# Attention with two gated layers: one line for all transfers in the planner, a later projection of head 1, and 1/z of seven head pairs spread by DMA

## The chip, the core and the metric

The kernel runs on one core of a Trainium2 chip. A core has TensorE (PE in the views; its weight loads are PEld), VectorE (DVE), ScalarE (ACT), GpSimd (POOL) and SyncE (SP), which issues transfers; ScalarE issues transfers as well. The metric is the device time of one execution in microseconds, taken as the median of repeated runs.

## The reference

Two batches of eight attention heads, 768 positions, head dimension 64, all in float32. A query sees a key only where six sign bits of a projection agree. The heads' outputs, side by side, go through two gated feed-forward layers.

```python
q_bits = (np.einsum('bhsd,dk->bhsk', q, proj) > 0)        # six bits
mask = q_bucket[:, :, :, None] == k_bucket[:, :, None, :]
scores = np.where(mask, scale * q @ k.T, -1e9)
attn = np.exp(scores - scores.max(-1, keepdims=True))
attn = attn / (attn.sum(-1, keepdims=True) + 1e-09)        # 1/z of each query
x = (attn @ v) laid out as [batch, seq, 512]
x = spatial_gating(x, w_in, w_spatial, b_spatial, w_out)   # first layer
out = x + relu(layernorm(x) @ w_ch1) @ w_ch2               # second layer
```

## The kernel before

**How work is put in order.** The kernel's code does not issue instructions. Each call (`nc.vector...`, `nc.sync.dma_start`) is recorded as a job in `Plan`, with its engine and what it must come behind. `Plan.run` then gives every job a modelled start, and `Plan.issue` writes the instructions of each engine in the order of these starts. The modelled numbers only set the order: on the chip each engine goes through its own list in order and waits on semaphores for what an instruction really needs. `plan.behind` adds an artificial "not ahead of this job". For transfers the model uses two tables, `LAND` (a fixed time by kind) and `RATE` (bytes per microsecond), and one queue for each of the two issuing engines.

**Stages.** The attention part goes over 96 tiles, each of 128 queries of one head (six tiles a head, two heads a pair, four pairs a batch). `attn_step` writes, for step i: the transposes of tile i (`pt`, six on PE), the scores of tile i+2 (`sc`, eight matmuls on PE: four chunks of two passes), the masked maximum of tile i+1 (`x`, on DVE), its exponent with the row sum z (ACT). A head's six tiles are closed by `po` (PE, weighted values), whose result goes to `xT`, one slice of 128 rows (two heads) by 768 queries for each pair. There are two score buffers in PSUM (`ps_s`) and four buffers for everything else (`ps_b`). `pair_load`, `mismatch` (PE products `pm` with `sides`, then the bits `m` on DVE), `pair_split` and `passes_of` prepare the operands `ks` and `qs` of the next head; `passes_of` puts them together by transfers on SP, partly from `m`. The layers' work is mixed into the last third of the attention part and follows it.

**Normalization.** `summed` takes 1/(z + 1e-9) of a pair in one tile `zr` (128 queries x 12: six query blocks by two heads). `normalized`, three tiles behind the last `po` of the pair, widens `zr` to 128x384 on POOL twice (`zw`), transposes it by six 128x128 matmuls into PSUM (`pz`), and multiplies `xT` by it on DVE, twice 128x384.

**Start.** `sides` holds the signed projection for head 0 in partitions 0 to 63 and for head 1 in 64 to 127, each made by three small DVE instructions from `pj`, loaded on ACT's queue. `mismatch(0, 0, slice(0, D))` projects head 0 alone, `first_parts` builds the operands of the first two query groups, and a second `mismatch(0, 0)` projects the whole pair for head 1. The first is `pm_0_151` and the second `pm_0_179` in the order below (`pm_0_203` after the change).

Of the kernel before, what the change touches and what calls it, by code (L numbers as in the profile page):

```python
# [169 lines left out]
class Plan:  # L170
# [15 lines left out]
    LAND = {"load": 2.0, "move": 1.5, "store": 1.5}  # L186
    RATE = {"load": 300e3, "move": 195e3, "store": 200e3}
# [111 lines left out]
    def run(self, late=None):  # L299
# [10 lines left out]
        queue = {e: 0.0 for e in engines}  # L310
# [42 lines left out]
        while todo:  # L353
# [38 lines left out]
            if j.bytes:  # L392
                other = "ACT" if e == "SP" else "SP"
                begin, span = max(queue[e], free[e] + self.LAND[j.way]), j.bytes / self.RATE[j.way]
                both = max(0.0, min(queue[other] - begin, 2 * span)) / 2
                if both:
                    queue[other] += both
                j.end = queue[e] = begin + span + both
# [113 lines left out]
def attn_moe_kernel(ctx: ExitStack, tc: tile.TileContext, qT, kT, v, proj, w_in, w_spT, b_sp, w_out, g_ln, w1, w2, out):  # L512
# [103 lines left out]
    nc.scalar.dma_start(out=pj[0:D], in_=proj)  # L616
    nc.scalar.dma_start(out=pj[D:P], in_=proj)
# [6 lines left out]
    for a, own in enumerate((slice(0, D), slice(D, P))):  # L624
        for i, sign in enumerate((1.0, -1.0, 1.0)):
            at = a * HROW + i * NB
            nc.vector.tensor_scalar(sides[own, at : at + NB], pj[own], sign, None, op0=ALU.mult)
    side = {"k": sides[:, NB : NB + QUAD], "q": sides[:, 0:QUAD]}
# [202 lines left out]
    def scores(b, h, g, j):  # L831
        jm = f"{b}_{h}_{g}_{j}"
        ks, qs = heads[b, h]["ks"], groups[b, h, g]["qs"]
        qsl = slice(j * P, (j + 1) * P)
        sc = ps_s.tile([P, 1024], F32, tag="sc", name=f"sc_{jm}")[:, :S]
        for csl in (slice(0, 512), slice(512, S)):
            for i, rows in enumerate((P, MR)):
                nc.tensor.matmul(
                    sc[:, csl], qs[:rows, i, qsl], ks[:rows, i, csl], start=(i == 0), stop=(i == 1)
                )  # L840
        tiles[b, h, g, j] = {"sc": sc}

    def masked_max(b, h, g, j):
# [15 lines left out]
        if (b, h, g, j) == (0, 0, 0, 0):  # L859
            pair_split(0, 0, first=True)  # L860
# [41 lines left out]
    def summed(b, r):  # L902

        zr = ap.tile([P, NQT, 2], F32, tag="zr", name=f"zr_{b}_{r}")
        nc.vector.tensor_scalar(zr, z_sum[b][:, :, 2 * r : 2 * r + 2], 1e-9, None, op0=ALU.add)
        nc.vector.reciprocal(zr, zr)
        pairs[b, r]["zr"] = zr

    def normalized(b, r):

        zr = pairs[b, r]["zr"]
        for c in range(2):
            zw = ap.tile([P, 6, D], F32, tag="zw", name=f"zw_{b}_{r}_{c}", bufs=2)
            zc = zr[:, c * 3 : c * 3 + 3, :].rearrange("p a (h o) -> p (a h) o", o=1)
            nc.gpsimd.tensor_scalar(zw, zc.to_broadcast([P, 6, D]), 1.0, 0.0, op0=ALU.mult, op1=ALU.add)
            pz = ps_b.tile([P, 3, P], F32, tag="b", name=f"pz_{b}_{r}_{c}")
            for i in range(3):
                nc.tensor.transpose(pz[:, i, :], zw[:, 2 * i : 2 * i + 2].rearrange("p h d -> p (h d)"), ident)
            xs = xT[b][:, r, c * KC : (c + 1) * KC]
            nc.vector.tensor_tensor(xs, pz.rearrange("p a n -> p (a n)"), xs, op=ALU.mult)  # L920

    def attn_step(i):
# [758 lines left out]
```

## Time and profile before

| | |
|---|---|
| median of 3 runs | 646.48 us (645.09 to 646.70) |
| time of the profiled execution | 645.79 us |
| its span, first to last instruction | 643.6 us |
| PE busy | 634.8 us (99%) |
| DVE busy | 500.4 us (78%) |
| ACT busy | 327.7 us (51%) |
| POOL busy | 189.6 us (29%) |

The profile is of one execution. The 2.2 us between its span and its time lie before the first and behind the last instruction. Nearly all instructions are recorded through one helper, so they carry one source line (L502) and are told apart by the names of their tiles, written out<-in.

### The profile page before, as it was taken

How to read it: one execution, taken by the hardware profiler on the slowest of the kernel's cores; microseconds unless marked ns; L12 is line 12 of the kernel's file. 1: busy time of each engine (PE TensorE's matmuls, PEld its weight loads, DVE VectorE, ACT ScalarE, POOL GpSimd, SP SyncE). 2: the span in 40 equal slices, each digit the busy share in tenths (PEclk: the TensorE clock that was granted, in tenths of full speed). 3: DMA queues.
4: the chain of work that ended last, by engine and by line, in shares of the span. 5: the costliest groups of instructions: out<-in, count | busy, mean ns of one | idle time of the engine just before them, and what ended most of it. 6: DMA issues, size and time to landing. Idle time of an engine off the chain costs nothing.

```text
span 643.6 us, 10095 instructions
## 1 busy us (share of the span) xinstructions
PE 634.8 (99%) x3506; PEld 520.3 (81%) x3506; DVE 500.4 (78%) x998; ACT 327.7 (51%) x650; POOL 189.6 (29%) x186
## 2 busy tenths in 40 slices
PE   7999999999999999999999999999999999999997
PEld 5777767777787777877888888899999899898896
DVE  6789878797888686886799544699998887969555
ACT  7888877885565655643555323554323333333110
POOL 2142433244554633131343200122122324142200
PEclk9999999999999999999999999999999999999999
DMA  6776676667767877774653240421262626382623
GB/s 153 195 206 155 181 181 154 183 145 240 204 181 243 235 195 212 228 264 176 231 167 145 73 148 17 147 86 46 99 231 114 234 92 223 105 279 74 218 88 143
DMA packets 64738, 107.68 MB, mean 167 GB/s; under 512 B 7008, under 2 KB 33328, under 8 KB 64432
## 3 DMA queue, kind: packets, MB, share of 16 engines
q1 hardware_dynamic: 43232, 67.58, 36.0%
q10 hardware_dynamic: 21456, 39.46, 18.5%
q8 instruction: 28, 0.46, 0.3%
q14 instruction: 22, 0.18, 0.1%
HBM read 63.31 MB, written 24.90 MB: 137 GB/s over the span
## 4 chain that ended last, share of the span: by engine, by line
PE 94%; DMA 2%; DVE 2%; issue 1%; SPq 0%; POOL 0%; ACTq 0%; DVEq 0%; POOLq 0%
PE acc L502 20%; PE p L502 14%; PE pv L502 10%; PE sc L502 10%; PE pt L502 10%; PE po L502 9%; PE pg L502 7%; PE pc L502 5%; PE py L502 5%; DMA qs<-q 2%; PE pm L502 1%; PE pz L502 1%; PE ptr_g L502 1%; PE px_c L502 1%; DMA pj<-in_proj 1%
## 5 line engine op out<-in xcount | busy, mean ns | idle before, releaser
L502 PE MATMUL acc<-w,ch 128*128 128x512 f32 x576 | 142.9, 393 | 0.0
L502 PEld LDWEIGHTS acc<-w,ch 128*128 128x128 f32 x576 | 107.3, 188 | 18.9
L502 ACT ACTIVATE x<-x,nb 128x768 f32<-128x768 f32 x96 | 89.7, 936 | 31.3 <-DVE x L502 26.4
L502 DVE TENSOR_SCALAR_CACHE_REDUCE x<-sc 128x768 f32<-128x768 f32 x96 | 90.9, 951 | 6.8 <-PE sc L502 3.7
L502 PE MATMUL sc<-ks,qs 128*128 128x512 f32 (+3 forms) x384 | 93.8, 363 | 1.9 <-DVE x L502 1.2
L502 POOL TENSOR_TENSOR f64c_w<-f_w,f64c_w 128x512 f32<-128x512 f32 x32 | 44.1, 1380 | 152.9 <-issue 81.8
L502 PE MATMUL pt<-ident,x 128*128 128x128 f32 x576 | 81.3, 274 | 0.3 <-DVE xT L502 0.3
L502 PEld LDWEIGHTS pt<-ident,x 128*128 128x128 f32 x576 | 66.5, 140 | 14.9 <-issue 2.4
L502 PEld LDWEIGHTS sc<-ks,qs 128*128 128x128 f32 (+1 forms) x384 | 62.9, 190 | 13.9 <-issue 2.2
L502 PE MATMUL po<-e,vv 128*64 128x384 f32 x384 | 65.5, 490 | 0.0
L502 ACT ACTIVATE ch<-u 128x384 fp32r<-128x384 f32 x48 | 25.2, 525 | 79.1 <-DVE u L502 67.0
L502 ACT ACTIVATE e<-pt 128x384 f32<-128x384 f32 x120 | 55.0, 485 | 18.6 <-PE pt L502 18.1
L502 DVE TENSOR_TENSOR u<-p,u 128x384 f32<-128x384 f32 x84 | 45.4, 552 | 20.5 <-PE p L502 20.0
L502 PEld LDWEIGHTS po<-e,vv 128*64 128x64 f32 x384 | 26.1, 137 | 31.2 <-issue 29.8
L502 PE MATMUL p<-t,w 128*128 128x384 f32 x252 | 50.0, 337 | 0.0
L502 PE MATMUL p<-xh,w 128*128 128x384 f32 x252 | 48.8, 338 | 0.0
L502 DVE COPY e<-pt 128x384 f32<-128x384 f32 x72 | 39.7, 553 | 9.6 <-PE pt L502 9.0
L502 PEld LDWEIGHTS p<-t,w 128*128 128x128 f32 x252 | 44.9, 188 | 2.3
L502 PEld LDWEIGHTS p<-xh,w 128*128 128x128 f32 x252 | 44.6, 188 | 2.2 <-DVE u L502 0.3
L502 POOL TENSOR_TENSOR w<-f64c_w,w 128x512 fp32r<-128x512 f32 (+1 forms) x28 | 35.2, 1259 | 37.8 <-ACT w L502 15.0
L502 DVE TENSOR_SCALAR f64c_w<-f64c_w 128x512 f32<-128x512 f32 x64 | 30.8, 480 | 18.5 <-ACT f64c_w L502 15.8
L502 PE MATMUL pg<-vn,w_sp 128*128 128x512 f32 x180 | 43.6, 396 | 0.0
(155 smaller groups left out, 1018.5 us busy)
## 6 DMA issues: line engine op xcount, KB each, us to landing
f_w<-in_w ACTq DMA_DIRECT2D x32, 512.0 KB
ots<-y_dram SPq DMA_DIRECT2D x12, 768.0 KB
ks<-k SPq DMA_DIRECT2D x45, 192.0 KB
y_dram<-ots SPq DMA_DIRECT2D x30, 256.0 KB
qs<-q SPq DMA_DIRECT2D x30, 192.0 KB
wst_sp<-in_w_spT SPq DMA_DIRECT2D x12, 384.0 KB
vv<-in_v SPq DMA_DIRECT2D x16, 192.0 KB
qs<-q SPq DMA_DIRECT2D x30, 96.0 KB
```

The costliest lines, as they stand in the source:

```text
L502: res = getattr(getattr(nc, engine[j.engine]), op)(*map(live, args), **{k: live(x) for k, x in kw.items()})
```

## The change

It has three parts.

1. In the planner, the two queues of transfers become one line that all transfers go through, with new fixed times and rates and a minimum of 0.1 us each. No instruction comes or goes by this; the order changes on every engine.
2. At the start, `sides` of head 1 is made behind the bits of head 0, and the second `mismatch(0, 0)` is recorded behind the scores of tile 1.
3. For seven of the eight pairs, `zr` is transposed as it is (one matmul, 12 rows by 128), copied to SBUF on DVE (`zt`), stored to DRAM (`zd`, 6 KB) and loaded again twice, each time one row of 768 spread over 64 partitions (`zb`, 192 KB each). `normalized` then multiplies once, 128x768 with both inputs in SBUF, eight tiles behind. The last pair keeps the old way three tiles behind. The buffer `zw`/`zb` goes from two of 128x384 to one of 128x768.

```diff
-    LAND = {"load": 2.0, "move": 1.5, "store": 1.5}
-    RATE = {"load": 300e3, "move": 195e3, "store": 200e3}
+    REACH = 1.15
+    LAND = {"load": 0.5, "move": 0.1, "store": 0.3}
+    RATE = {"load": 270e3, "move": 218e3, "store": 270e3}
...
-                other = "ACT" if e == "SP" else "SP"
-                begin, span = max(queue[e], free[e] + self.LAND[j.way]), j.bytes / self.RATE[j.way]
-                both = max(0.0, min(queue[other] - begin, 2 * span)) / 2
-                if both:
-                    queue[other] += both
-                j.end = queue[e] = begin + span + both
+                line = max(line, free[e] + self.REACH) + max(j.bytes / self.RATE[j.way], 0.1)
+                j.end = line + self.LAND[j.way]
...
-    for a, own in enumerate((slice(0, D), slice(D, P))):
+
+    def sides_of(a, behind=None):
+        own = slice(a * D, (a + 1) * D)
+        nc.scalar.dma_start(out=pj[own], in_=proj)
+        plan.behind = behind
         for i, sign in enumerate((1.0, -1.0, 1.0)):
             at = a * HROW + i * NB
             nc.vector.tensor_scalar(sides[own, at : at + NB], pj[own], sign, None, op0=ALU.mult)
+        plan.behind = None
+
+    sides_of(0)
...
         if (b, h, g, j) == (0, 0, 0, 0):
+            plan.behind = tiles[0, 0, 0, 1]["job"]
+            mismatch(0, 0)
+            plan.behind = None
             pair_split(0, 0, first=True)
...
-        zr = ap.tile([P, NQT, 2], F32, tag="zr", name=f"zr_{b}_{r}")
-        nc.vector.tensor_scalar(zr, z_sum[b][:, :, 2 * r : 2 * r + 2], 1e-9, None, op0=ALU.add)
+        zr = ap.tile([P, 2, NQT], F32, tag="zr", name=f"zr_{b}_{r}")
+        for h in range(2):
+            nc.vector.tensor_scalar(zr[:, h], z_sum[b][:, :, 2 * r + h], 1e-9, None, op0=ALU.add)
         nc.vector.reciprocal(zr, zr)
         pairs[b, r]["zr"] = zr
+        if (b, r) == (B - 1, H // 2 - 1):
+            return
+        rows = 2 * NQT
+        pz = ps_b.tile([P, GW], F32, tag="b", name=f"pz_{b}_{r}")
+        nc.tensor.transpose(pz[:rows, :P], zr.rearrange("p h a -> p (h a)"), ident)
+        zt = ap.tile([rows, P], F32, tag="zt", name=f"zt_{b}_{r}", bufs=1)
+        nc.vector.tensor_copy(zt, pz[:rows, :P])
+        zd = dram.tile([2, 1, S], F32, tag=f"zd_{b}_{r}", name=f"zd_{b}_{r}")
+        nc.sync.dma_start(out=zd.rearrange("h o (a q) -> (h o a) q", a=NQT), in_=zt)
+        zb = ap.tile([P, S], F32, tag="zw", name=f"zb_{b}_{r}", bufs=1)
+        for h in range(2):
+            nc.sync.dma_start(out=zb[h * D : (h + 1) * D], in_=zd[h].to_broadcast([D, S]))
+        pairs[b, r]["zb"] = zb
...
+        if "zb" in pairs[b, r]:
+            nc.vector.tensor_tensor(xT[b][:, r], pairs[b, r]["zb"], xT[b][:, r], op=ALU.mult)
+            return
...
-        for late, e in ((1, summed), (3, normalized)):
+        for late, e in ((1, summed), (3, normalized), (8, normalized)):
             n = i - PO - late
+            if late > 1 and (late == 8) == (n == NT - 1):
+                continue
...
-    plan.behind = made
-    mismatch(0, 0)
-    plan.behind = None
+    sides_of(1, made)
```

**PE and DVE at the start.** On PE, before the change, the second projection stands ahead of the first scores:

```order
L502 MATMUL pm_0_151<-raws,sides 32x384 x4
L502 MATMUL warm<-ident 128x128 x10
L502 MATMUL pm_0_179<-raws,sides 32x384 x4
L502 MATMUL sc_0_0_0_188<-ks_0_0_145,qs_0_0_149 128x512 x2
L502 MATMUL sc_0_0_0_188<-ks_0_0_145,qs_0_0_149 128x256 x2
L502 MATMUL sc_0_0_1_196<-ks_0_0_145,qs_0_0_149 128x512 x2
L502 MATMUL sc_0_0_1_196<-ks_0_0_145,qs_0_0_149 128x256 x2
L502 MATMUL sc_0_0_2_215<-ks_0_0_145,qs_0_0_149 128x512 x2
```

On PE, after the change (L499 is the same helper):

```order
L499 MATMUL pm_0_151<-raws,sides 32x384 x4
L499 MATMUL warm<-ident 128x128 x10
L499 MATMUL sc_0_0_0_181<-ks_0_0_143,qs_0_0_148 128x512 x2
L499 MATMUL sc_0_0_0_181<-ks_0_0_143,qs_0_0_148 128x256 x2
L499 MATMUL sc_0_0_1_193<-ks_0_0_143,qs_0_0_148 128x512 x2
L499 MATMUL sc_0_0_1_193<-ks_0_0_143,qs_0_0_148 128x256 x2
L499 MATMUL pm_0_203<-raws,sides 32x384 x4
L499 MATMUL sc_0_0_2_212<-ks_0_0_143,qs_0_0_148 128x512 x2
```

The projection of head 1 moved from ahead of tile 0 to between tiles 1 and 2. On DVE, before, all six instructions for `sides` come first, and the second bits `m_0_199` ahead of the first maximum:

```order
L502 TENSOR_SCALAR sides<-pj 64x6 x6
L502 TENSOR_TENSOR ks_0_0_145<-raws,ks_0_0_145 64x768
L502 TENSOR_SCALAR m_0_167<-pm_0_151,above,worth 128x384
L502 SCALAR_TENSOR_TENSOR qs_0_0_149<-dup,qs_0_0_149 64x384
L502 CAST ks_0_0_145<-m_0_167 12x384
L502 SCALAR_TENSOR_TENSOR qs_0_384_177<-dup,qs_0_384_177 64x384
L502 TENSOR_SCALAR m_0_199<-pm_0_179,above,worth 128x384
L502 TENSOR_SCALAR x_0_0_0_208,nb_0_0_0_207<-sc_0_0_0_188 128x768
L502 TENSOR_SCALAR x_0_0_1_212,nb_0_0_1_211<-sc_0_0_1_196 128x768
L502 SCALAR_TENSOR_TENSOR k_0_0_191<-raws,k_0_0_191 128x768
```

On DVE, after:

```order
L499 TENSOR_SCALAR sides<-pj 64x6 x3
L499 TENSOR_TENSOR ks_0_0_143<-raws,ks_0_0_143 64x768
L499 TENSOR_SCALAR m_0_164<-pm_0_151,above,worth 128x384
L499 SCALAR_TENSOR_TENSOR qs_0_0_148<-dup,qs_0_0_148 64x384
L499 CAST ks_0_0_143<-m_0_164 12x384
L499 TENSOR_SCALAR sides<-pj 64x6 x3
L499 SCALAR_TENSOR_TENSOR qs_0_384_174<-dup,qs_0_384_174 64x384
L499 TENSOR_SCALAR x_0_0_0_197,nb_0_0_0_196<-sc_0_0_0_181 128x768
L499 TENSOR_SCALAR x_0_0_1_209,nb_0_0_1_208<-sc_0_0_1_193 128x768
L499 TENSOR_SCALAR m_0_217<-pm_0_203,above,worth 128x384
L499 SCALAR_TENSOR_TENSOR k_0_0_177<-raws,k_0_0_177 128x768
```

Three of the `sides` moved behind the first operands, and the second bits (`m_0_217`) behind two maxima.

**PE at the normalization of pair 0.** Before:

```order
L502 MATMUL pt_2_1_1_1_664<-ident,x_2_1_1_602 128x128 x3
L502 MATMUL sc_3_0_0_658<-ks_3_0_490,qs_3_0_548 128x256 x2
L502 MATMUL pz_0_0_672<-ident,zw_0_0_534 128x128 x3
L502 MATMUL pz_0_1_677<-ident,zw_0_1_546 128x128 x3
L502 MATMUL sc_3_0_1_685<-ks_3_0_490,qs_3_0_548 128x512 x2
```

After:

```order
L499 MATMUL pt_2_0_2_0_609<-ident,x_2_0_2_536 128x128 x3
L499 MATMUL pt_2_0_2_1_618<-ident,x_2_0_2_536 128x128 x3
L499 MATMUL pz_0_622<-ident,zr_0_482 12x128
L499 MATMUL sc_2_1_2_625<-ks_2_0_352,qs_2_384_465 128x512 x2
L499 MATMUL sc_2_1_2_625<-ks_2_0_352,qs_2_384_465 128x256 x2
```

One matmul stands where six stood.

**SP at a change of pairs.** These are SP's transfers for the first head of the second pair of batch 1 (`ks_2`, `qs_2`), before:

```order
L502 DMA ks_2_0_1731<-k_1_1_1654 64x768 x2
L502 DMA qs_2_0_1774<-q_1_1_1656 64x2x384
L502 DMA qs_2_0_1774<-m_1_1777 12x384
L502 DMA ks_2_0_1731<-m_1_1777 12x384
L502 DMA ks_2_0_1731<-k_1_1_1654 64x768
L502 DMA qs_2_0_1774<-q_1_1_1656 64x384
L502 DMA ks_2_0_1731<-m_1_1777 12x384
```

And after:

```order
L499 DMA ks_2_0_1700<-k_1_1_1629 64x768
L499 DMA zd_3_1716<-zt_3_1706 12x128
L499 DMA ks_2_0_1700<-k_1_1_1629 64x768
L499 DMA zb_3_1751<-zd_3_1716 64x768 x2
L499 DMA ks_2_0_1700<-m_1_1760 12x384
L499 DMA qs_2_0_1784<-q_1_1_1633 64x2x384
L499 DMA qs_2_0_1784<-m_1_1760 12x384
L499 DMA qs_2_0_1784<-q_1_1_1633 64x384
L499 DMA ks_2_0_1700<-k_1_1_1629 64x768
L499 DMA ks_2_0_1700<-m_1_1760 12x384
```

The store of 1/z of the pair before and its two loads now stand among them, ahead of five or six transfers of the next head.

## Rows read from the trace of the kernel before

**Rows 1.** The page: busy time of each engine, share of the span, instructions.

```profile
PE 634.8 (99%) x3506; PEld 520.3 (81%) x3506; DVE 500.4 (78%) x998; ACT 327.7 (51%) x650; POOL 189.6 (29%) x186
PEclk9999999999999999999999999999999999999999
```

**Rows 2.** The page: share of the chain that ended last, by engine.

```profile
PE 94%; DMA 2%; DVE 2%; issue 1%; SPq 0%; POOL 0%; ACTq 0%; DVEq 0%; POOLq 0%
```

**Rows 3.** PE's waits in the whole span: for whom, us, times, longest.

```profile
PE warm L502 <- POOL above L502: 1.4, 1, 1.4
PE pm L502 <- DVE qs L502: 1.3, 1, 1.3
PE sc L502 <- DVE x L502: 1.2, 2, 0.9
PE sc L502 <- DMA qs<-q: 0.5, 1, 0.5
PE pt L502 <- DVE xT L502: 0.3, 1, 0.3
PE sc L502 <- PE pt L502: 0.2, 1, 0.2
```

**Rows 4.** Tile pz (ns min/median/max, first and last start), and its piece of the chain.

```profile
L502 PE MATMUL pz<-ident,zw x48: 269/273/330, 46.6 to 302.6; 128*128 128x128 f32 x48
L502 DVE TENSOR_TENSOR xT<-pz,xT x16: 547/552/558, 47.9 to 303.7; 128x384 f32<-128x384 f32 x16
...
46.72 0.66 PE pz L502 x6
```

**Rows 5.** Timeline of the first 12 us: start, us, engine, instruction, [idle before, releaser].

```profile
4.00 0.84 ACT L502 ACTIVATE ks<-raws 64x768 fp32r<-64x768 f32 x1 [0.46 <-DMA raws<-in_kT]
...
5.61 0.32 DVE L502 TENSOR_SCALAR sides<-pj 64x6 f32<-64x6 f32 x3 [0.94 <-DMA pj<-in_proj]
...
5.96 0.95 DVE L502 TENSOR_TENSOR ks<-raws,ks 64x768 fp32r<-64x768 f32 x1
6.31 0.52 ACT L502 ACTIVATE qs<-dup 64x384 fp32r<-64x384 f32 x1 [0.49 <-DMA dup<-in_qT]
...
7.00 0.83 POOL L502 TENSOR_SCALAR ks<-dup 64x768 fp32r<-64x768 f32 x1 [3.56 <-DVE ks L502]
...
8.30 0.68 POOL L502 CAST qs<-m 12x384 fp32r<-12x384 f32 x1 [0.47 <-DVE qs L502]
8.33 0.85 PE L502 MATMUL pm<-raws,sides 128*32 128x384 f32 x8 [1.25 <-DVE qs L502]
...
9.11 1.68 PE L502 MATMUL sc<-ks,qs 128*128 128x512 f32 x8
...
10.08 0.68 DVE L502 TENSOR_SCALAR m<-pm,above,worth 128x384 fp32r<-128x384 f32 x1
...
10.67 0.95 DVE L502 TENSOR_SCALAR_CACHE_REDUCE x<-sc 128x768 f32<-128x768 f32 x1
...
11.69 1.68 PE L502 MATMUL sc<-ks,qs 128*128 128x512 f32 x6 [0.90 <-DVE x L502]
```

**Rows 6.** Tile q: DVE's split of a pair's queries, both inputs in SBUF.

```profile
L502 DVE SCALAR_TENSOR_TENSOR q<-q x7: 924/1494/1589, 24.1 to 220.1; 128x768 fp32r<-128x768 f32 x7
```

**Rows 7.** Timeline near 94 us: load of a next pair, product of `pz`, later maximum.

```profile
94.11 0.43 SPq L502 DMA_DIRECT2D q<-in_qT  x1
...
100.59 0.95 DVE L502 TENSOR_SCALAR_CACHE_REDUCE x<-sc 128x768 f32<-128x768 f32 x1
```

**Rows 8.** SP and PE at the change of pairs shown above, and DMA in it.

```profile
132.11 0.80 SPq L502 DMA_DIRECT2D qs<-m  x1
...
134.49 0.51 SPq L502 DMA_DIRECT2D qs<-q  x1
135.06 0.78 SPq L502 DMA_DIRECT2D ks<-m  x1
...
139.61 0.96 PE L502 MATMUL sc<-ks,qs 128*128 128x512 f32 x4
...
132.00:134.00 2.00, 2.00 (x18) 1.77 (x18) 2.00 (x4) 1.50 (x4) 1.65 (x2) 1.00 1.02 296
```

**Rows 9.** A transfer on the chain, issue to release of PE.

```profile
26.91 5.21 DMA qs<-q
```

More of the change, by code (lines that the diff above doesn't have):

```diff
@@ L309, in run @@
         free = {**{e: 0.7 for e in engines}, "POOL": 1.7}
-        queue = {e: 0.0 for e in engines}
+        line = 2.85
         ready = {j: 0.0 for j in jobs}
@@ L615, in attn_moe_kernel @@
     pj = const.tile([P, NB], F32, name="pj")
-    nc.scalar.dma_start(out=pj[0:D], in_=proj)
-    nc.scalar.dma_start(out=pj[D:P], in_=proj)
     HROW = 3 * NB
@@ L840, in scores @@
                 )
-        tiles[b, h, g, j] = {"sc": sc}
+        tiles[b, h, g, j] = {"sc": sc, "job": plan.jobs[-1]}
     def masked_max(b, h, g, j):
@@ L909, in normalized @@
+        for h in range(2):
+            nc.sync.dma_start(out=zb[h * D : (h + 1) * D], in_=zd[h].to_broadcast([D, S]))
+        pairs[b, r]["zb"] = zb
     def normalized(b, r):
+        if "zb" in pairs[b, r]:
+            nc.vector.tensor_tensor(xT[b][:, r], pairs[b, r]["zb"], xT[b][:, r], op=ALU.mult)
+            return
         zr = pairs[b, r]["zr"]
+        both = ap.tile([P, S], F32, tag="zw", name=f"zw_{b}_{r}", bufs=1)
         for c in range(2):
-            zw = ap.tile([P, 6, D], F32, tag="zw", name=f"zw_{b}_{r}_{c}", bufs=2)
@@ L914, in normalized @@
-            zc = zr[:, c * 3 : c * 3 + 3, :].rearrange("p a (h o) -> p (a h) o", o=1)
-            nc.gpsimd.tensor_scalar(zw, zc.to_broadcast([P, 6, D]), 1.0, 0.0, op0=ALU.mult, op1=ALU.add)
+            zw = both[:, c * KC : (c + 1) * KC].rearrange("p (a h d) -> p a h d", a=3, h=2)
+            for h in range(2):
+                zc = zr[:, h, c * 3 : c * 3 + 3].rearrange("p (a o) -> p a o", o=1)
+                nc.gpsimd.tensor_scalar(zw[:, :, h], zc.to_broadcast([P, 3, D]), 1.0, 0.0, op0=ALU.mult, op1=ALU.add)
@@ L916, in normalized @@
             pz = ps_b.tile([P, 3, P], F32, tag="b", name=f"pz_{b}_{r}_{c}")
             for i in range(3):
-                nc.tensor.transpose(pz[:, i, :], zw[:, 2 * i : 2 * i + 2].rearrange("p h d -> p (h d)"), ident)
+                nc.tensor.transpose(pz[:, i, :], zw[:, i].rearrange("p h d -> p (h d)"), ident)
             xs = xT[b][:, r, c * KC : (c + 1) * KC]
```

## The prediction

> **What bounds the kernel now.** I read the page's busy row first: TensorE (PE) is busy 634.8 us, 99% of the span, and the row of the granted clock shows its top step in all 40 slices, so no time is to be had from the clock [rows 1]. The chain of what ended last says the same from the other side: 94% of it is PE, and no other engine or DMA has more than 2% [rows 2]. Then I listed whom PE waited for [rows 3]. All six waits add up to 4.9 us, and 3.9 us of these (1.4 for the warm-up, 1.3 and 1.2) belong to the first 17 us. For the rest of the span PE waits 0.5 + 0.3 + 0.2 = 1.0 us in all. This settles how the change must be costed. What only reorders transfers or relieves POOL and DVE has 1.0 us to win at most. Work taken from PE counts in full, work added elsewhere counts nothing as long as PE isn't made to wait, and the start is to be costed by itself.
>
> The profiled execution took 645.79 us, 2.2 us above its span; the sum is made against 645.79. The median of the runs is 646.48, 0.7 us above it. A difference under 0.3%, 1.9 us, is about what this kernel's measurements can't tell from no change; I call that "the same".
>
> **The matmuls of 1/z.** Before, `pz` is 48 matmuls, six a pair, each some 0.27 us long, but overlapped: the six on the chain take 0.66 us, 0.11 us each [rows 4]. After, seven pairs have one and the last pair keeps six: 13. So 35 go, 35 x 0.11 = **-3.85 us**. The new one streams the same 128 columns of `ident` and has 12 rows of output where it had 128. I price it at the same 0.11; were it free, 0.8 us more would go; a matmul that came out alone at its whole 0.27 us would give back 7 x 0.16 = 1.1 us.
>
> **The start.** DVE stood 0.94 us for `pj` and then made the three `sides` of head 1 in 0.32 us, before it took `ks` at 5.96. ACT's `ks`, its other input, had ended at 4.84. So `ks` can start 1.1 us earlier and end near 5.8. Next comes POOL's `ks` from `dup` (0.83 us), which had started at 7.00 behind it; the load of `dup` that ACT waited for until 6.31 may now be the later one. Then POOL ends near 7.1, its cast of `qs` (0.68) near 7.9, and the first scores start near 8.0 where they started at 9.11; the projection's 0.85 us no longer lies ahead of them [rows 5]. That projection isn't saved: it is PE work that goes between tiles 1 and 2, into the 0.90 us that PE waited for the first `x`. What gives some of it back is DVE. Its `m` of head 1 (0.68) now stands behind two maxima, its first `x` can't start before a tile of scores is there, and the second head's operands, which hang on `m`, get later against an earlier PE. The two old waits behind this part, 1.3 and 1.2 us, are the most there is [rows 3]. Bounds: 0 (PE arrives earlier and waits longer) and -1.1. I take the middle, **-0.6**.
>
> **DVE's product.** It was 2 x 0.55 us a pair with one input in PSUM [rows 4]. Now it is one 128x768 with both inputs in SBUF. No row shows that product; the nearest is the split of `q`, the same shape with both inputs in SBUF: 0.92 at the least, median 1.49, at most 1.59 us [rows 6]. So a pair costs between -0.18 and +0.49 us of DVE, to which the copy `zt` (bounds: nothing, and the 0.55 of a 128x384; its 12x128 should be near the lower end) and one more small `zr` are added. I take +0.6 us a pair, 4 us in all. DVE has 643.6 - 500.4 = 143 us free, 18 a pair, and this hides it [rows 1]. Uncovered it would cost 7 x 0.6 = 4.2 us, the whole gain; I take nothing, since PE waited for DVE for 0.3 us in all behind the start [rows 3].
>
> The row of `q` bears on a rule: one shape takes 0.92 or 1.59 us. The Trainium skill ("GPSIMD Engine Reference", Specifications) says that GpSimd and VectorE share their ports to SBUF, and that a VectorE instruction with two SBUF inputs is one that contends. The spread in the row agrees, and the rule speaks against the new product. By it each product is a slow one, which is what the +0.49 above already has.
>
> **The new transfers.** SP gets three a pair, 21 in all. Its issues took 0.43 to 0.80 us [rows 7, 8], so 2 us a pair. Two of them write 192 KB each, 393 KB; at the 296 GB/s that the rows of the change of pairs show, the line is taken for 1.33 us [rows 8]. Two places could make someone wait.
>
> - The product behind `zb`. It stands on DVE far behind the issue. In the stretch that I laid out, the issue comes right behind the next pair's load at 94.11, at about 95, and the product's place is behind the maximum at 100.59 [rows 7]. That is some 6 us; the transfer on the chain took 5.21 from issue to landing [rows 9]. So DVE doesn't wait, by about 1 us. If it does, behind the product in DVE's order stand the next `x`, which PE's `pt` needs, and the mask bits of the next head.
> - The loads of the next head. At the change of pairs shown, `zd` (0.8) and two `zb` (1.2 of issues, 1.33 of line) come ahead of five or six of its transfers. Up to 3.3 us are added there. Before, the last `ks<-m` was issued at 135.06 and the scores that read it began at 139.61, 4.55 us later, 3.8 behind the end of the issue [rows 8]. Its own landing lies in that time too, so a transfer pushed back by the whole 3.3 us would be late. But PE waited 0.5 us in all for such a transfer, on one occasion [rows 3], and SP's order begins some of them earlier. I take nothing, and up to 0.5 us a pair, 3.5 us, as the other bound.
>
> `zd` also holds SP: if it must wait for `zt`, all issues behind it wait. `zr` comes one tile behind the last `po`, and PE and DVE run close to their orders, so I take nothing; the last rival below has the price.
>
> **POOL and the order.** POOL loses `zw` for seven pairs. Nobody waited for POOL but the warm-up [rows 3], so this is worth nothing, and it is also why the widening that moves from POOL to transfers can't gain by itself. The new order of all engines, from the planner's one line, can at most take the 1.0 us of later waits, or add new ones; I take 0. The end is left as it was, since the last pair keeps its way.
>
> **Sum.** 645.79 - 3.85 - 0.6 = 641.3 on the profiled execution's footing; with the 0.7 between it and the median, 642.0. The free part of `pz` (0.8, above) and the 1.0 of later waits lie on the low side and the 1.1 of a lone matmul on the high side; I take 0.3 of the balance and forecast **641.7 us**.
>
> **Rivals.**
>
> - *Forecast, 0.58.* `pz` pays in full, the start in part: 641.7, with a range of its own from 640.5 to 643.
> - *The start gives nothing, 0.12.* The first scores come 1 us earlier and PE waits it off at tiles 2 and 3 for `x` and the second `m`. 641.7 + 0.6 = 642.3.
> - *More than the sum, 0.10.* The one line orders the transfers so well that the later 1.0 us goes as well, and the start gives 1.1: 641.7 - 1.0 - 0.5 = 640.2. For it: the 0.5 for a transfer is the largest of the later waits [rows 3]. Against it: more is put on the line, not less.
> - *The gain is eaten, 0.13.* Either each slow product stands uncovered in front of an `x` (7 x 0.55 = 3.8 us), or the loads of the next head come 0.5 us late at each pair (3.5). 641.7 + 3.6 = 645.3, the same. The contention of the two engines' ports as the Trainium skill has it (the page and section named above) would be the first of these. Against both: the waits of PE before are so few that there must be slack, but I can't read from them how much.
> - *Slower, 0.07.* One mechanism: an engine held in its order. DVE stands at the product until `zb` has landed, or SP at `zd` until `zt` is there, with `ks` and `qs` behind. It decides, making the kernel slower than before by 1.9 us, from (3.85 + 0.6 + 1.9) / 7 = 0.9 us a pair. At 1.0 us a pair: 641.7 + 7.0 = 648.7. For it: the product's margin is only about 1 us by the rows that I have, and the transfer of 5.21 us was a smaller one than `zb`. Against it: two maxima a pair would have to go by without a buffer of scores or `x` to cover, and PE has two buffers of scores.
>
> **How the numbers follow.** The likeliest case gives 641.7. On the low side the range takes in the case of "more" and the free `pz`: 639.5. On the high side it reaches to the eaten gain, 645.6, and leaves out the slower case and some of each tail. Faster by over 0.3% means below 644.5, which the first three cases are: 0.80. The eaten gain is the same: 0.13. Slower, above 648.4, is the last: 0.07.
>
> **What would show it right or wrong.** `pz` must have 13 matmuls, with seven of 12 rows. PE's busy time should fall by about 4 us, to near 631, with no more idle time than before behind the start. The first scores should start near 8.0, and the projection with 0.85 us stand at the end of tile 1's scores. In PE's waits there should be no new row with `xT`, `x` or a transfer above a microsecond. DVE should show no wait for a transfer of `zb`, and SP none for `zt` with `ks` or `qs` late behind. The product should take 0.92 to 1.59 us. I am wrong if PE's busy time falls as said and its idle time grows by the same: then the list of its waits names which of the two places it was. I am also wrong if `pz` falls to 13 and PE's busy time doesn't move, for then the six overlapped with neighbours and weren't worth 0.11 each.

## The result and the profile after

The changed kernel takes 649.50 us (median of 8 runs, 647.49 to 651.06) against 645.65 us for the kernel before: a ratio of 1.006, with a 95% interval from 1.0048 to 1.0071, so 3.9 us slower. The profiled execution took 647.49 us, its span 645.7; it is the fastest of the eight, so about 2 us of the median's loss are in no trace of this kernel. Two of the eight, 650.67 and 651.06, have a mean granted clock of 0.997, where the others have 0.999 or 1.000.

First the page of the changed kernel, the rows of busy time and of the chain by engine ([rows 1, 2] before):

```profile
PE 633.5 (98%) x3471; PEld 515.8 (80%) x3471; DVE 507.9 (79%) x1006; ACT 325.5 (50%) x650; POOL 183.5 (28%) x174
PE 82%; DVE 9%; DMA 3%; ACT 2%; issue 2%; POOL 1%; SPq 0%; ACTq 0%; POOLq 0%; DVEq 0%
```

PE's busy time fell by 1.3 us, not 4, DVE's rose by 7.5, and DVE holds 9% of the chain where it held 2%. The 7.5 are not mainly the new product: by the page the conversions `f64c_w` alone went from 30.8 to 36.4 us with the same instructions, and `e2_start` below, which has no such product, has DVE busy for 509.2 us. Whom PE waited for, in the whole span ([rows 3] before):

```profile
PE sc L499 <- DVE x L499: 2.3, 6, 0.8
PE sc L499 <- DMA qs<-q: 2.2, 2, 1.4
PE warm L499 <- POOL above L499: 1.5, 1, 1.5
PE pt L499 <- ACT xT L499: 1.0, 1, 1.0
PE sc L499 <- DVE qs L499: 0.8, 1, 0.8
PE p L499 <- DVE u L499: 0.2, 1, 0.2
PE sc L499 <- POOL qs L499: 0.2, 1, 0.2
PE pt L499 <- ACT x L499: 0.2, 1, 0.2
```

That is 8.4 us in place of 4.9. The tiles of part 3 (`pz`, `zt`, `zb`), with ns min/median/max, and what DVE's products waited for ([rows 4] before):

```profile
L499 PE MATMUL pz<-ident,zr x7: 272/273/274, 42.6 to 258.3; 128*12 128x128 f32 x7
L499 PE MATMUL pz<-ident,zw x6: 272/273/330, 302.8 to 303.4; 128*128 128x128 f32 x6
...
L499 DVE COPY zt<-pz x7: 268/274/274, 43.7 to 259.4; 12x128 f32<-12x128 f32 x7
...
L499 DVE TENSOR_TENSOR xT<-zb,xT x7: 942/957/960, 100.3 to 280.8; 128x768 f32<-128x768 f32 x7
...
DMA zb<-zd: 2.7, 4
```

The instructions are as said: 13 matmuls, a product of 0.95 us. DVE stood 2.7 us for `zb`, in four of seven products. The start, from the timeline ([rows 5] before):

```profile
7.85 0.68 POOL L499 CAST qs<-m 12x384 fp32r<-12x384 f32 x1 [0.47 <-DVE qs L499]
...
7.93 0.47 PE L499 MATMUL sc<-ks,qs 128*128 128x512 f32 x1 [0.75 <-DVE qs L499]
...
8.59 1.46 PE L499 MATMUL sc<-ks,qs 76*128 76x512 f32 x7 [0.18 <-POOL qs L499]
...
9.98 0.85 PE L499 MATMUL pm<-raws,sides 128*32 128x384 f32 x8
...
15.46 0.73 PE L499 MATMUL sc<-ks,qs 128*128 128x512 f32 x2 [0.77 <-DVE x L499]
```

The first scores start at 7.93 (forecast: 8.0), and their second pass at 8.59, behind POOL's cast. And one place at 104 us, where PE comes to the second half of the queries of head 7 (heads counted from 0 over both batches), SP and PE, with the transfer on the chain that PE waited for:

```profile
97.39 1.31 SPq L499 DMA_DIRECT2D qs<-q  x2
...
100.87 0.50 SPq L499 DMA_DIRECT2D zd<-zt  x1
101.47 2.60 SPq L499 DMA_DIRECT2D zb<-zd  x2
104.35 0.64 SPq L499 DMA_DIRECT2D qs<-q  x1
...
104.77 0.47 PE L499 MATMUL sc<-ks,qs 128*128 128x512 f32 x1 [1.43 <-DMA qs<-q]
...
98.11 6.52 DMA qs<-q
```

The transfer took 6.52 us where the one on the chain before took 5.21 [rows 9], with `zd` and two `zb` on the line behind it, and PE stood 1.43 us. Head 7's first scores had started at 97.23, where they started at 99.38 before; behind the wait, at 104.77, PE is level with before (104.79). So 2.1 us of lead were lost within one head.

### The profile page after: what moved, and what is told of

The parts are those of the page before. It is cut to its first block, busy times and chain, and to the rows that moved or that the text cites. A ratio compares the mean times of both kernels' runs of the same rounds, so it can differ in the third digit from the quotient of the medians.

```text
span 645.7 us, 10073 instructions
## 1 busy us (share of the span) xinstructions
PE 633.5 (98%) x3471; PEld 515.8 (80%) x3471; DVE 507.9 (79%) x1006; ACT 325.5 (50%) x650; POOL 183.5 (28%) x174
## 4 chain that ended last, share of the span: by engine, by line
PE 82%; DVE 9%; DMA 3%; ACT 2%; issue 2%; POOL 1%; SPq 0%; ACTq 0%; POOLq 0%; DVEq 0%
PE acc L499 17%; PE p L499 13%; PE pv L499 10%; PE sc L499 8%; PE po L499 8%; PE pg L499 8%; PE pt L499 8%; PE py L499 5%; DMA qs<-q 3%; PE pc L499 2%; DVE x L499 2%; DVE rx L499 1%; PE ptr_g L499 1%; PE pm L499 1%; DVE t L499 1%
## 5 line engine op out<-in xcount | busy, mean ns | idle before, releaser
L499 PE MATMUL acc<-w,ch 128*128 128x512 f32 x576 | 142.8, 392 | 0.0
L499 PEld LDWEIGHTS acc<-w,ch 128*128 128x128 f32 x576 | 107.3, 188 | 19.3
L499 ACT ACTIVATE x<-x,nb 128x768 f32<-128x768 f32 x96 | 89.7, 937 | 27.0 <-DVE x L499 18.1
L499 PE MATMUL sc<-ks,qs 128*128 128x512 f32 (+3 forms) x384 | 93.7, 363 | 5.5 <-DVE x L499 2.3
L499 DVE TENSOR_SCALAR_CACHE_REDUCE x<-sc 128x768 f32<-128x768 f32 x96 | 90.6, 949 | 5.5 <-PE sc L499 2.4
L499 POOL TENSOR_TENSOR f64c_w<-f_w,f64c_w 128x512 f32<-128x512 f32 x32 | 43.5, 1360 | 153.6 <-issue 64.4
L499 PE MATMUL pt<-ident,x 128*128 128x128 f32 x576 | 81.0, 274 | 1.3 <-ACT xT L499 1.0
L499 PEld LDWEIGHTS sc<-ks,qs 128*128 128x128 f32 (+1 forms) x384 | 63.2, 190 | 21.3 <-DVE x L499 4.9
L499 PEld LDWEIGHTS pt<-ident,x 128*128 128x128 f32 x576 | 66.6, 141 | 13.2 <-ACT e L499 2.2
L499 ACT ACTIVATE e<-pt 128x384 f32<-128x384 f32 x120 | 55.1, 487 | 26.5 <-PE pt L499 24.7
L499 ACT ACTIVATE ch<-u 128x384 fp32r<-128x384 f32 x48 | 25.1, 526 | 81.8 <-DVE u L499 81.5
L499 PE MATMUL po<-e,vv 128*64 128x384 f32 x384 | 65.5, 490 | 0.0
L499 DVE TENSOR_TENSOR u<-p,u 128x384 f32<-128x384 f32 x84 | 45.0, 550 | 16.6 <-PE p L499 16.0
L499 PEld LDWEIGHTS po<-e,vv 128*64 128x64 f32 x384 | 26.1, 137 | 31.3 <-issue 29.3
L499 PE MATMUL p<-t,w 128*128 128x384 f32 x252 | 50.2, 339 | 0.0
L499 PE MATMUL p<-xh,w 128*128 128x384 f32 x252 | 49.1, 338 | 0.2 <-DVE u L499 0.2
L499 PEld LDWEIGHTS p<-t,w 128*128 128x128 f32 x252 | 44.5, 188 | 2.8 <-DVE u L499 0.8
L499 PEld LDWEIGHTS p<-xh,w 128*128 128x128 f32 x252 | 44.6, 188 | 2.6 <-DVE u L499 0.5
L499 DVE COPY e<-pt 128x384 f32<-128x384 f32 x72 | 39.3, 551 | 7.1 <-PE pt L499 6.7
L499 PE MATMUL pg<-vn,w_sp 128*128 128x512 f32 x180 | 43.8, 396 | 0.0
L499 POOL TENSOR_TENSOR w<-f64c_w,w 128x512 fp32r<-128x512 f32 (+1 forms) x28 | 33.4, 1195 | 33.5 <-ACT w L499 15.1
L499 DVE TENSOR_SCALAR f64c_w<-f64c_w 128x512 f32<-128x512 f32 x64 | 36.4, 568 | 6.5 <-ACT f64c_w L499 6.1
```

What stands on the lines that cost most here:

```text
L499: res = getattr(getattr(nc, engine[j.engine]), op)(*map(live, args), **{k: live(x) for k, x in kw.items()})
```

## The experiments

All figures are ratios of the medians to the kernel before on the same chip, with a 95% interval, times its 646 us. The prediction had PE as the bound. Four theories were tried against each other. **A**: the new transfers push the next head's operands back. **B**: the order that the one line makes is worse. **C**: any newly made order costs some us on the chip, whatever the planner's model thinks of it. **D**: what is added sets the time, and the order is nothing special.

**The three parts alone, and the change without its transfers.** `e1_line` has only part 1, `e2_start` only part 2, `e3_spread` only part 3 of the diff shown above, each in the order that the planner then makes.

> The kernel before with the planner's one line for all transfers alone (part 1 of the change): same instructions, another order. Theory A (the loss comes from the new transfers zd and zb, which push the next head's operands back): within 0.5 us of before, 645 to 646.5, with the waits of PE behind the start as few as before. Theory B (the loss comes from the order that the one line makes): 3 to 6 us above before, 649 to 652, with new waits of PE for x and for qs<-q, as in the changed kernel.

> The kernel before with part 2 alone (sides of head 1 and the second projection later). Both theories: first scores about 1.1 us earlier. If PE keeps what is won there, 0.6 to 1.1 us below before; if the later x gives it back, within 0.3 us of before.

> The kernel before with part 3 alone (1/z of seven pairs spread by DMA), in the order that the old table makes of it. Theory A: slower than before by 2 to 5 us, with waits of PE for qs<-q and of DVE for zb, though 35 matmuls are gone. Theory B: 3 to 4 us faster than before, 642 to 643.

`e4_no_transfers` keeps the changed kernel's order:

```diff
                 for op, args, kw in j.calls:
+                    if j.left_out:
...
+                            nc.gpsimd.memset(ones, 1.0)
+                        continue
+                    if j.by_one:
+                        args = (args[0], ones, args[2])
```

> The changed kernel with its order on every engine kept, but none of the 21 transfers zd and zb issued; the products read a tile of ones, so the output lacks 1/z of seven pairs. Theory A: what the transfers cost comes back, 642 to 645. Theory B: the order costs the same without them, 648 to 650, with the waits of PE for x still there.

Measured: `e1_line` 1.0026 (1.0018 to 1.0034), +1.7 us. `e2_start` 1.0046 (1.0032 to 1.006), +3.0. `e3_spread` 1.0059 (1.0044 to 1.0074), +3.8. `e4_no_transfers` 1.0017 (1.0 to 1.0035), +1.1. Each part loses by itself, the start too, for which neither theory had a loss. By number, `e3_spread` is as A said, and `e1_line` and `e4_no_transfers` lie between A and B. The three sum to 8.5 and the change costs 3.9, so they don't add up. The 21 transfers are worth 3.9 - 1.1 = 2.8 us in the changed order (1.4 to 4.1 with both intervals): by the middle figure A explains more than half of the loss, not all, and B (3 to 6 us) is too large. In the trace of `e4_no_transfers` PE has no wait from 95 to 112 us. The profiled execution took 649.91 us, 2.7 above its median, and its longest wait is elsewhere, at the first scores of head 2:

```profile
PE sc L507 <- DMA ks<-m: 2.1, 1, 2.1
```

**Orders that change nothing else.** Two kernels with the instructions of before and one number of the planner's model moved by a few per cent.

```diff
-    NEXT = 0.03
+    NEXT = 0.032
```

> The kernel before with the planner's NEXT at 0.032 in place of 0.03: the same instructions, nothing of the change, but 143 of 904 instructions of DVE in other places. Theory C (each of the three parts costs mostly because any new plan of the same quality in the model loses a few waits on the chip that the order before happens not to have): 1 to 3 us above before, 647 to 649, with one to four new waits of PE of about a microsecond. Theory D (the order before is nothing special, and the parts cost by what they add): within 0.5 us of before.

> The same with SLACK at 2.1 in place of 2.0, which moves 158 of 904 instructions of DVE. Theory C: 1 to 3 us above before. Theory D: within 0.5 us of before.

Measured: 1.0033 (1.0021 to 1.0045), +2.1 us, and 1.0117 (1.0104 to 1.013), +7.6 us, more than C said. D's "nothing special" falls: of two orders that no reason speaks against, both are slower than the one before. So a part that makes the planner start anew can't be read by its content alone, and the next kernels hold the order before and move only the instructions of one part, by hand.

**The parts in the order before.**

```diff
+        for at, new in self.moved.items():
+            self.jobs[at].start = self.jobs[new].start + 1e-4 * (at + 1)
         order = sorted((j for j in self.jobs if j.engine), key=lambda j: (j.part, j.start, j.at))
...
+    plan.moved.update({7: 47, 8: 47, 9: 47, 54: 60, 55: 73})
```

> Part 2 of the change put by hand into the order before: three sides, four matmuls of the second projection and its bits move, every other instruction keeps its place. Theory C: faster than before by 0 to 1.1 us, where part 2 with a new plan was 2.8 slower. Theory D: about as slow as that, 648 to 649.

```diff
+        for j in (zw0, xt0, zw1, pz1, xt1):
+            j.calls = []
+        pz0.calls = [("transpose", (pz[:rows, 0, :], zr.rearrange("p h a -> p (h a)"), ident), {})]
...
+        more("SP", xt0, 0.4, "dma_start", {"out": Once(lambda: zd().rearrange("h o (a q) -> (h o a) q", a=S // 128)), "in_": Once(lambda: zt()[:])})
...
+        more("DVE", xt0, 8.9, "tensor_tensor", {"out": xs, "in0": Once(lambda: zb()[:]), "in1": xs, "op": ALU.mult})
```

> Part 3 of the change put by hand into the order before: one transpose in the place of the first three, zt and zd right behind it, zb 2.5 us behind zd, the product some 9 us behind; every other instruction keeps its place. Theory C: the 35 matmuls pay, 642 to 643.5. Theory A (the transfers push the next head's operands back): 646 to 650, with waits of PE for qs<-q.

Measured: `e7_held_start` 1.0018 (1.0008 to 1.0028), +1.2 us; `e8_held_spread` 1.0116 (1.0102 to 1.013), +7.5. Neither theory's number came for either (`e8_held_spread` is above A's range as well). Both contents lose without any new order, so C isn't the whole either. In `e7_held_start` (timeline, DVE and PE) PE is 1.1 us earlier at the first scores, and waits 1.5 us in two places by 19 us, which the view puts down to maxima (the second is taken up at `e16_held_start_two`); DVE has the first of these maxima behind the later `m` and the splits of `k` and `q`, which stand between:

```profile
8.05 0.47 PE L505 MATMUL sc<-ks,qs 128*128 128x512 f32 x1 [0.32 <-DVE qs L505]
...
11.78 0.68 DVE L505 TENSOR_SCALAR m<-pm,above,worth 128x384 fp32r<-128x384 f32 x1
...
14.11 0.95 DVE L505 TENSOR_SCALAR_CACHE_REDUCE x<-sc 128x768 f32<-128x768 f32 x1
...
15.12 1.61 PE L505 MATMUL sc<-ks,qs 128*128 128x512 f32 x6 [0.79 <-DVE x L505]
...
18.96 0.96 PE L505 MATMUL sc<-ks,qs 128*128 128x512 f32 x4 [0.67 <-DVE x L505]
```

In `e8_held_spread` the "slower" rival happened in full. DVE stood 7.3 us for `zb` in four products. The longest of these, in the timeline, and PE's longest wait, 8 us later, for a copy of DVE (that the one made all of the other is not shown):

```profile
228.49 0.96 DVE L544 TENSOR_TENSOR xT<-zb,xT 128x768 f32<-128x768 f32 x1 [2.93 <-DMA zb<-zd]
...
236.89 1.14 PE L544 MATMUL pt<-ident,x 128*128 128x128 f32 x6 [2.90 <-DVE xT L544]
```

**The spread with the product later, and without its transfers.** `e9_held_later` moves two numbers of `e8_held_spread`, the product's place (below) and that of `zb`, from 2.9 to 5.9 us; `e10_held_no_transfers` drops `zd` and `zb` from `e8_held_spread` and keeps its product 9 us behind.

```diff
-        more("DVE", xt0, 8.9, "tensor_tensor", {"out": xs, "in0": Once(lambda: zb()[:]), "in1": xs, "op": ALU.mult})
+        more("DVE", xt0, 11.4 if name == "0_3" else 18.0, "tensor_tensor", {"out": xs, "in0": Once(lambda: zb()[:]), "in1": xs, "op": ALU.mult})
```

(The "42 transfers" in the first of the next two texts is a slip for the 21 above.)

> As e8, with the two loads of zb 3 us later and the product 9 us later (for the last pair of batch 0, whose reader is near, 1 and 2.5 us later). If the loss of e8 was DVE held at the product and SP held at zd's landing: 643 to 646, with no wait of DVE for zb. If the 42 transfers of part 3 cost by their load on the line or on SP wherever they stand: 648 to 653.

> The order before with 35 matmuls less and the one product of 128x768, but without zd and zb: the products read ones, so the output lacks 1/z of seven pairs. This prices the matmuls by themselves. If each is worth 0.11 us: 641.8 to 642.8. If PE gets them back as waits at the next x or operand: 644.5 to 647.

Measured: `e9_held_later` 1.0076 (1.0057 to 1.0095), +4.9 us; `e10_held_no_transfers` 1.0013 (1.0004 to 1.0022), +0.8. So the 21 transfers cost 7.5 - 0.8 = 6.7 us in the order before with the product 9 us behind, DVE's waits for `zb` included. `e9_held_later` is 4.1 us above `e10_held_no_transfers`, but the two differ in the product's place as well. DVE's waits for `zb` are down from 7.3 to 0.8 us in it; PE now waits for operands and for the engines that feed it (three of the longest waits of `e9_held_later`):

```profile
PE sc L544 <- DVE x L544: 2.0, 6, 1.0
PE sc L544 <- DMA ks<-k: 1.6, 1, 1.6
PE pt L544 <- DVE xT L544: 1.6, 1, 1.6
```

And `e10_held_no_transfers` shows that 35 matmuls less, with DVE's new work and no transfers, win nothing. One place where its gain went, at 229 us: first the kernel before, then `e10_held_no_transfers` (timeline).

```profile
229.47 1.14 PE L502 MATMUL pt<-ident,x 128*128 128x128 f32 x6 [0.30 <-DVE xT L502]
```

```profile
227.64 0.89 DVE L545 TENSOR_SCALAR f64c_w<-f64c_w 128x512 f32<-128x512 f32 x2 [1.97 <-POOL w_sp L545]
...
230.27 0.56 DVE L545 COPY xT<-po 64x384 f32<-64x384 f32 x1
...
230.89 1.13 PE L545 MATMUL pt<-ident,x 128*128 128x128 f32 x6 [1.33 <-DVE xT L545]
```

The copy `xT<-po` that PE needs stands in DVE's order behind conversions of weights, which wait for other engines (in the kernel before too, 2.27 us for the same `w_sp`). PE's wait there grew from 0.30 to 1.33.

**Two other orders of the changed kernel**, with the numbers of `e5_placebo_next` and `e6_placebo_slack`.

> The changed kernel with NEXT at 0.032 in place of 0.03: another order, the same work. Theory C (plans scatter by some us on the chip, and the changed kernel has one of them): 645 to 655, at least 1 us away from 649.5. Theory D (the content sets the time): 649 to 650.

> The changed kernel with SLACK at 2.1 in place of 2.0. Theory C: 645 to 655, at least 1 us away from 649.5 or from the run above. Theory D: 649 to 650.

Measured: 1.0065 (1.0053 to 1.0077), +4.2 us, and 1.007 (1.0048 to 1.0091), +4.5. That is within a microsecond of the change's +3.9. C's "at least 1 us away" did not come, and the medians of 650.3 and 650.0 miss D's 649 to 650 by 0.3 us at most. In three orders of the changed kernel the loss is about the same, so it is not one bad order.

**DVE's order at two places.**

```diff
+        for at, new in ((562, 492), (1305, 1268), (1306, 1268), (1307, 1268)):
+            self.jobs[at].start = self.jobs[new].start + 1e-6 * at
```

> As e10 (order before, 35 matmuls less, products by ones, no transfers), with four conversion instructions of DVE moved behind the copies that PE waits for, at the two places where e10 gave most back (0.7 us at 87 us, 1.15 us at 229 us). If the matmuls' gain was given back at such places, where DVE's order holds a copy behind a conversion that waits for a load: 644.5 to 645.3, 1.1 to 1.9 us below e10. If it is only given back at the next place: within 0.5 us of 646.4.

Measured: 0.9999 (0.9988 to 1.001), 0.9 us below `e10_held_no_transfers` by the ratios, with intervals that overlap. It lies between the two theories. PE's wait of 1.33 us at 229 us is not in its trace any more; that some of the gain comes back there is likely, but by the times hardly clear of the noise, and where the rest is given back is not shown by this run.

**What PE's time is worth.** 42 matmuls more in the attention part, 14 fewer in the second layer, and part 2 with one maximum earlier.

```diff
+        for j in self.twice:
+            j.calls = j.calls * 2
```

> The order before, with the 42 transposes pz of seven pairs run twice each: 42 matmuls more in the attention part. At the face value of 0.11 us: 4.6 us above before, 650.3. If PE's time there has slack against the other chains that e10 met, 0 to 3 us above before.

```diff
+                    if n % 30 or c[2].get("start") or c[2].get("stop"):
+                        keep.append(c)
+                j.calls = keep
```

> The order before, with 14 of the 576 matmuls acc of the second layer left out (its sums lack them), 0.227 us each from start to start, 3.2 us in all, behind 400 us. If PE is the bound there: 642.2 to 643. If the conversions of weights meet PE there as well: 644 to 646.

```diff
-    plan.moved.update({7: 47, 8: 47, 9: 47, 54: 60, 55: 73})
+    plan.moved.update({7: 47, 8: 47, 9: 47, 54: 60, 55: 73, 86: 63})
```

> As e7 (part 2 in the order before), with the maximum of tile 2 put ahead of the split of q, where e7's PE waited 0.8 us for it at 15 us; the changed kernel has it so. If that wait is what turned part 2's gain into a loss: 644.5 to 645.6, at or below before. If the operands of head 1 are late as well: 646 to 647.

Measured: `e14_matmuls_twice` 1.005 (1.0035 to 1.0064), +3.2 of the 4.6 us; `e15_layers_less` 0.9966 (0.9954 to 0.9978), -2.2 of the 3.2; `e16_held_start_two` 1.0019 (1.001 to 1.0028), +1.2, as `e7_held_start`, and above what was expected of it. So the late maximum of tile 2 alone was not part 2's loss.

The traces show what most of it is, at the first scores of head 1 (tile 6). SP issues that head's operands in order, `ks<-m` ahead of `qs<-q`. First the kernel before, then `e7_held_start`, whose scores stand above at 18.96:

```profile
11.60 1.70 SPq L502 DMA_DIRECT2D ks<-m  x2
...
14.94 0.54 SPq L502 DMA_DIRECT2D qs<-q  x1
...
18.10 0.96 PE L502 MATMUL sc<-ks,qs 128*128 128x512 f32 x4
```

```profile
12.49 1.71 SPq L505 DMA_DIRECT2D ks<-m  x2
...
15.84 0.54 SPq L505 DMA_DIRECT2D qs<-q  x1
```

`m` ends at 12.46 there, and SP issues `ks<-m` right behind it and all that follows 0.9 us later than before. The scores start 3.1 to 3.2 us behind the issue of `qs<-q` in both, in `e16_held_start_two` (15.59 and 18.77) and in `e15_layers_less` (15.07 and 18.24). The maximum of tile 5, which the view names at 18.96, is not what they need: in the kernel before it ran from 17.96 to 18.91, and the scores started at 18.10. So the late operands of head 1 put PE 0.9 us behind in `e7_held_start` and 0.7 in `e16_held_start_two`, of the 1.2 that either loses. In `e2_start`, with an order of its own, these scores start at 17.97, no later than before, so its 3.0 us lie elsewhere.

`e15_layers_less` has another use: up to 400 us it is the kernel before, instruction by instruction, so its trace is a second look at it. PE's waits there, from 17 to 400 us:

```profile
PE pt L511 <- ACT xT L511: 0.7, 1, 0.7
PE pm L511 <- DMA k<-in_kT: 0.6, 1, 0.6
PE sc L511 <- PE pt L511: 0.6, 1, 0.6
PE pt L511 <- ACT x L511: 0.3, 1, 0.3
```

These are 2.2 us, where the profile of before had 1.0, and mostly for other releasers. At 140.61 it starts the scores that start at 139.61 in the profile of before.

**The matmuls alone and DVE's part alone**, in the order before.

```diff
+        for pz, product, c, args in self.fewer:
...
+            pz.calls = pz.calls[:1] if c == 0 else []
+            product.calls = [("tensor_tensor", args, {"op": ALU.mult})]
```

> The order before with 35 transposes pz left out and nothing else: widening on POOL and both products of 128x384 stay, each product reading the one transpose that is left (so 1/z of seven pairs is wrong). At face value (0.11 us each): 3.85 below before, 642.3. At the two thirds that e14 and e15 found for added and removed matmuls: 2.6 below, 643.6. If PE's time before pairs of heads is worth nothing, as e10 read: within 0.8 us of before.

```diff
+            one.calls = [("tensor_copy", (), {"out": zt, "in_": pz[:12, 0, :]})]
+            two.calls = []
...
+            j.calls = [("tensor_tensor", (), {"out": xs, "in0": xs, "in1": xs, "op": ALU.mult})]
```

> The order before with DVE's part of the change alone: for seven pairs the copy zt of 12x128 in the place of the first product, and one product of 128x768 from SBUF (xT by itself, so the output is wrong) 18 us behind; all 48 transposes and the widening stay, no transfers. If e10 lost the matmuls' gain to DVE's new product: 1.5 to 3.5 us above before. If not: within 0.8 us of before.

Measured: `e17_matmuls_alone` 0.9987 (0.9976 to 0.9998), -0.8 us; `e18_product_alone` 1.0026 (1.0017 to 1.0036), +1.7. They sum to +0.9, and `e10_held_no_transfers` was +0.8, but that the parts add up is not shown by it: `e18_product_alone` has the product 18 us behind and `e10_held_no_transfers` 9, and only the first keeps the widening. One of its seven products met a product of GpSimd and took 2.07 us, where the others took 0.94 to 0.96 (in `e10_held_no_transfers` all seven took 0.94 to 0.95):

```profile
139.05 1.55 POOL L522 TENSOR_TENSOR f64c_u<-f_u,f64c_u 128x512 f32<-128x512 f32 x1 [4.54 <-DVE f64c_out L522]
...
139.35 2.07 DVE L522 TENSOR_TENSOR xT<-xT 128x768 f32<-128x768 f32 x1
```

So a part of the 1.7 us may be this meeting; how much isn't measured.

The same seven pairs cost 3.2 us more when their matmuls double and give 0.8 back when they go. Where they give it back can be seen at the second half of head 7's queries. First the kernel before, then `e17_matmuls_alone`:

```profile
103.83 1.20 PE L502 MATMUL pt<-ident,x 128*128 128x128 f32 x9
104.79 0.95 PE L502 MATMUL sc<-ks,qs 128*128 128x512 f32 x4
```

```profile
103.75 1.20 PE L507 MATMUL pt<-ident,x 128*128 128x128 f32 x9
105.94 0.94 PE L507 MATMUL sc<-ks,qs 128*128 128x512 f32 x4 [1.00 <-DMA qs<-q]
```

The transfer was issued at 99.20 in the kernel before, and PE did not wait. It was issued at 99.29 here and at 99.80 in `e15_layers_less`, and the scores start at 105.94 and 105.79: PE's lead of 0.7 us over `e15_layers_less` at the transposes (103.75 for 104.44) is gone behind the transfer, though `zd` and `zb` are not there. By 141.02, where the kernel before is at 139.61 and `e15_layers_less` at 140.61, the 20 matmuls left out so far have won nothing. The last transposes `pz` start at 302.5, in the other two traces at 302.6 and 303.9: the 15 behind 141 us (1.65 at 0.11 each) won 1.5 against the one and 1.8 against the other.

No kernel here that computes the whole was faster than the one before.

## Why the prediction was wrong, by its steps

- **What bounds the kernel: the step that failed.** "Work taken from PE counts in full, work added elsewhere counts nothing as long as PE isn't made to wait." I read the few waits of PE [rows 3] as slack in everyone else. In this order other chains (the operands on the line of transfers, DVE's maxima and copies, the conversions) arrive at many places just when PE does, and there an earlier PE waits: 35 matmuls less gave 0.8 of 3.85 us (e17; 0.1 to 1.6 by its interval), with nothing up to 141 us and about all behind it in that trace; 42 more cost 3.2 of 4.6 (e14). That other chains meet PE is shown by the waits above; a margin for each chain wasn't measured. One profile was also too little to read 1.0 us from (2.2 in the second look, e15).
- **The matmuls of 1/z.** The count was right: 13 are left, and the six of the last pair are as before. So were the 0.11 us as time of PE: 42 more raise its busy time from 634.8 to 639.3, 0.11 each. The worth was 0.8, not 3.85. PE's busy time fell by 1.3 us (1.5 in e17), between the two signs of being wrong that I had named. The row cannot settle more: the same 3506 matmuls have 634.8 us in the trace of before and 638.1 in that of e5.
- **The start.** The first scores came at 7.93 for a forecast of 8.0, in part by luck: POOL's cast, which was to end at 7.9 ahead of them, ends at 8.53 and holds only their second pass. Behind them the forecast was wrong: "the second head's operands get later" had 0 as its worst bound, as if PE could only lose its lead. With `m` behind two maxima these operands come 0.9 us later than before (e7), so PE ends up later, and part 2 costs 1.2 us in the order before (e7, e16). It costs 3.0 when the planner makes a new order (e2), where these operands are not late.
- **DVE's product.** Its size was 0.95 us, at the low end of the range that I gave it, not at the median of 1.49. With `zt` (0.27) it is 0.1 us a pair more than the two of 0.55 that went, where I took 0.6. Its part costs 1.7 us all the same (e18, a part of it perhaps from the one product that met GpSimd), a term that I had hidden in 143 us of free time. Free time as a mean says nothing of the places where PE waits for a result that stands behind the new product in DVE's order.
- **The new transfers.** I took 0 and gave 3.5 us as the other bound. They cost 6.7 us in the order before with the product 9 us behind (e8 against e10), and 2.8 in the changed one (e4). This was the second half of the rival "the gain is eaten"; but there was hardly a gain to eat. The margin of the product, "about 1 us", was as thin as said: DVE waited in four of seven, 2.7 us in all, and where the product stood 9 us behind it was held for 7.3 (e8).
- **The order.** I took 0 for the planner's one line. It costs 1.7 us alone (e1), and two orders made by a small change of one number in the planner's model cost 2.1 and 7.6 (e5, e6).
- **The sum in place of mine**, in the order before: part 3 as a whole 4.9 or 7.5 us, by where its loads and its product stand (e9, e8), and part 2 1.2: +6.1 or +8.7 us. The changed kernel loses 3.9, so its own order gives back 2 us or more of it. Which of its moves do so is open, as is why e6's order is so bad, and what the median has above the profiled execution, beyond the lower clock of two runs.

The rule of the Trainium skill that I had weighed gave a rival by itself: the product from SBUF would contend with GpSimd and each be slow ("GPSIMD Engine Reference", Specifications). The trace of the changed kernel is no test of it: GpSimd ran nothing beside any of the seven products, which took 0.942 to 0.960 us. Where they did meet, this case agrees with it. GpSimd's product in `e18_product_alone` ended at 140.60, and DVE's at 141.42. Of the seven splits of `q` before [rows 6], the two with GpSimd idle took 0.92 and 0.96 us, and the five that started while GpSimd was in a product of `k` took 1.20 to 1.59. Those five and the product in `e18_product_alone` all ended 0.81 to 0.82 us behind the end of GpSimd's instruction. Not every overlap slowed DVE: a product of `e18_product_alone` that started 0.12 us behind GpSimd's, at 183.19, took 0.94. So the rival did not come because the two did not meet in the changed kernel; that they never contend does not follow.

## What to carry to other kernels

An engine at 99% with few waits, in an order written by a planner, is not proof that the others have slack: it may be that all chains were brought to meet, and then time taken from the busiest engine is worth a fraction (0.2 of it in the attention part here, 0.7 in the layers), while what was added to other chains here was paid for. Before a change that re-plans the order is judged, time one or two orders with no change in them: here they alone cost 2.1 and 7.6 us, where the gain that was hoped for was 4.5. To price one part, hold the order and move only that part's instructions.

## What the hardware showed that was not expected

- After PE had stood 2.9 us in `e8_held_spread`, its granted clock fell from 1.00 (2.4 GHz) to 0.51 in a later window (the level of 1.2 GHz nearly all of the time) and 0.64 in the next. It fell in the same way behind the 2.1 us in `e4_no_transfers` (0.52 from 34 to 36 us) and behind 2.7 us in `e11_changed_placebo_next` (0.56 from 94 to 96 us). So such a wait can cost more than its own time; how much more isn't measured. Windows of 2 us in `e8_held_spread`, busy time by engine (PE first), then PE's clock:

```profile
236.00:238.00 2.00, 1.07 (x7) 0.83 (x8) 1.94 (x5) 0.38 (x1) 0.00 (x0) 1.00 0.86 227
238.00:240.00 2.00, 2.00 (x10) 1.83 (x9) 2.00 (x5) 1.66 (x3) 0.00 (x0) 0.51 0.43 151
```

- A store of 6 KB held the queue behind it for long, since the loads of `zb` wait for it on SP: in `e8_held_spread` SP stood 10.4 us for `zd` to land, six times, up to 5.1.

```profile
SPq L544 <- DMA zd<-zt: 10.4, 6, 5.1
```

The Trainium skill ("DMA: Bandwidth & Descriptors", Anatomy of one DMA) gives about 2 us of fixed time for a transfer, measured there on GpSimd's path, most of it for the confirmation from memory. The wait of 5.1 us is above it; here the line was shared with other transfers (239 and 313 GB/s from 216 to 220 us, in that wait).

- PE's pace at the start differs from execution to execution. The ten matmuls `warm` at 6 us took 1.31 us in the trace of before and in fifteen others, and 2.39 or 2.40 in four (e1, e4, e5, e13), with 1.00 in the clock's row both times; in e1, e5 and e13 the first scores start 1.2 us later than before. In e13 this is gone by 32.31 us, where the scores of head 2 start (32.26 before). What it adds to a whole run isn't shown, and how often it comes in the runs without a profile isn't known.
